# The last step of the first network: its function cut into three chunks, its adds moved, and the order of three engines written out up to the second network

## The chip, the cores and the metric

The kernel runs on one core of a Trainium2 chip, in one launch. The metric is the device time of that core in microseconds (us), as the median of several executions. The engines named here are TensorE (PE, matrix products into PSUM; its weight loads are shown as PEld), VectorE (DVE), ScalarE (ACT), GpSimd (POOL) and SyncE (SP, which issues the DMAs).

## The reference

Three stages run one behind the other: an attention with random features over 2 batches, 8 heads, 576 positions; a first network; a second network. Its output, 1152 tokens of 512 values, goes through

```python
def _moe_ref(x, w_in, w_out):          # x 1152 x 512, w_in 512 x 2048, w_out 2048 x 512
    h = x @ w_in
    g = h - np.tanh(h)
    return (g @ w_out).astype(np.float32)

def _moe2_ref(x, domain_probs, w1, w2): # 4 experts, w1 512 x 1024, w2 1024 x 512
    p = domain_probs / (domain_probs.sum(-1, keepdims=True) + 1e-09)
    for e in range(E):
        h = np.maximum(x @ w1[e], 0.0)
        out += p[:, e:e + 1] * (h @ w2[e])
```

All products need near float32 precision. The kernel splits each operand into a high part in the fp32r format and a low part (operand minus high part), and adds three products for one: high by high, high by low, low by high.

## The kernel before

**First network.** Tokens lie along the free axis, 1152 wide, in three chunks of 384 (`NC = 3`, `CH = 384`). The 2048 hidden values are 16 blocks of 128, four units (i) of four blocks (j). For a block, `hidden` makes 36 matmuls into one PSUM tile `psh` of three banks (one bank a chunk). `activated` then computes h - tanh(h) from `psh` as ten operations, named by letters: on ScalarE `u` (h squared), `q`, `t` (tanh), `m` (mask of small h), `h` (high part `hh`); on VectorE `a`, `b` (a polynomial for small h), `s` (h - tanh h, in place in PSUM), `c` (the predicated copy that takes the polynomial where the mask is 0 or not), `l` (low part `hl`). Each of them runs over all 1152 tokens. `out_a(i, c, n)` makes the 12 matmuls that a unit adds to output rows c (of 4), tokens n (of 3), into a PSUM tile `po`; the function that it returns adds `po` to `acc` on VectorE (L550). There are two `po` buffers, so a third product waits for the add of the first.

**The loop.** Step n of twelve issues the hidden block `sh` (units 1 to 3) and the output row block `so` (of the unit before), three `out_a`. In the last step `sh` is block (3, 3) and `so` is (2, 3). Around it run the function of the block before, here (3, 2), and the weights' split: `Decoded` weights of this network arrive as float64, `y` and `m` on ScalarE (L111, L117) and two operations on VectorE (L126, L127) make a float32 `m` of them, ScalarE its high part and GpSimd its low part `wbl`. In this loop the order on VectorE, ScalarE and TensorE is the order in which the code emits (`manual_schedule`); in the last step the first two adds (`o[:1]`, `o[1:2]`) stand around the predicated copy `c`, as in all steps.

**Behind the loop.** The function of block (3, 3) runs whole. Of the last unit's twelve products the first five are begun with three of their four blocks (`last[:5]`): three in a spare `psh` tile, one bank each, two in `po`. When `hh` and `hl` of (3, 3) are there, the five get their last three matmuls each, all five in a row. Then the hand-written order ends. What comes next is placed by the framework's scheduler: the five adds, the split of `acc` into the second network's input (`x2`: high part on ScalarE, low part on VectorE, chunk by chunk), the other seven products, the first hidden blocks of the second network (`psh<-y`, weights `wah` and `wal` split from `raw` by ScalarE and VectorE), sums of tokens T1 to T4 (L568, `token_sums`), weights' sums (L598). The scheduler may move these up into the loop where an engine has room: the four weight splits `wah`, `wal` stand in the steps before, and 11 matmuls of the second network stand ahead of the sixth output product.

**Second network.** Experts' blocks 0 and 1 are plain (`hidden`, `activated`, `out_b` at L665); from the third pair on a Strassen scheme runs, hand-ordered again. The change doesn't touch it.

Of the kernel before, what the change touches and what calls it, by code (L numbers as in the profile page):

```python
# [8 lines left out]
F32 = mybir.dt.float32  # L9
F32R = mybir.dt.float32r  # L10
# [16 lines left out]
def tile_favor_attention__then__two_moe(  # L27
# [46 lines left out]
    def run(todo):  # L74
        for step in todo:
            step()
# [21 lines left out]
    class Decoded:  # L98
# [30 lines left out]
        def parted(self):  # L129
            hi, lo = halves_of(wp, self.tag)  # L130
            split(hi, lo, self.m.bitcast(F32), nc.gpsimd)
            return hi, lo
# [339 lines left out]

    def early(e):
# [224 lines left out]
    def opened(w):  # L698
        for x, _, _ in w:
            x.scaled()  # L700
            x.topped()
# [4 lines left out]
    with tc.manual_schedule(engines={mybir.EngineType.DVE, mybir.EngineType.PE, mybir.EngineType.Activation}):  # L706
# [3 lines left out]
        for n, (sh, so) in enumerate(order):  # L710
            now, coming = coming, loads(n + 1)
            g0 = g
            run(g0[x] for x in "uqt" if g0)
            edge = so % NJ == 0 and g0 is not None
# [11 lines left out]
            else:  # L726
                o, late_h = [], sh == END - 1
                run(H if late_h else H[:2])
                for c in range(NC):
                    o.append(out_a(*steps[so], c))  # L730
                    run(H[2 + c:3 + c] if not late_h else [])
                run(J[:1] + W[:1] + left + T("a") + T("m") + T("b") + T("s") + o[:1] + T("c") + T("h"))
                run(J[1:] + W[1:] + o[1:2] + T("l"))
            left = o[2:]
            g = activated(*steps[sh])
            opened(coming)
        last = [(c, n) for n in range(NC) for c in range(KD)]
        spare = late["ps_ha"].tile([P, NC, 512], F32, tag="h", name="psh")
        run(g[x] for x in "uqt")
        coming[0][0].joined()  # L740
        parted(*coming[0])
        run(left + [g[x] for x in "amb"])
        for k, (c, n) in enumerate(last[:5]):
            out_a(NA - 1, c, n, range(NJ - 1), spare[:, k] if k < NC else None)
        run(g[x] for x in "schl")
        ends = {(c, n): out_a(NA - 1, c, n, [NJ - 1]) for c, n in last[:5]}
    for f in range(2):
        ready(load_a, wa, NA, f)
    x2 = [[xp.tile([P, N], F32R, tag=f"x{a}{c}", name=f"y{a}{c}") for a in range(2)] for c in range(KD)]
    for n in range(NC):  # L750
        s = slice(n * CH, (n + 1) * CH)
        for c in range(KD):
            (ends.get((c, n)) or out_a(NA - 1, c, n))()
            split(x2[c][0][:, s], x2[c][1][:, s], state["acc"][:, c, s])
        if n == 1:
            state["x"] = x2
            for j in range(2):
                hidden(NA, j, [0])
# [155 lines left out]
```

## Time and profile before

| | us |
|---|---|
| median of 3 runs (lowest, highest) | 685.01 (684.14, 686.36) |
| the profiled execution | 686.23 |
| its span | 684.4 |
| TensorE busy | 668.2 (98%) |
| VectorE busy | 528.5 (77%) |
| ScalarE busy | 317.2 (46%) |
| GpSimd busy | 61.3 (9%) |

The span is from the first to the last instruction on the core; 1.8 us of the profiled execution lie outside it. TensorE is busy nearly all the time, so it is read by the few places where it waits. A timeline row gives the start, the time, the engine, the line and operation, the output tile and the inputs, the number of instructions of the row, and in brackets the idle time before it and what ended it. Matmuls overlap: the time of one (0.34 us for 384 columns) is longer than the distance from one start to the next (0.173 us).

### The profile page before, as it was taken

The page shows a single profiled execution, that of the slowest core. Times are in us where ns is not written, and L with a number is a line of the kernel's source. Part 1 is how long each engine was busy: PE and PEld are TensorE (multiplying, and loading weights), DVE is VectorE, ACT ScalarE, POOL GpSimd, SP SyncE. Part 2 cuts the span into 40 slices and gives each one's busy share as a digit, 9 for nine tenths or more (in the row PEclk, how much of TensorE's full clock was granted, in tenths as well). Part 3 has the DMA queues.
Part 4 walks back from the last instruction along what each step waited for, and adds up shares of the span by engine and source line. Part 5 has one row for each costly group of instructions (what it writes and reads, how often), then busy time and mean ns, then how long its engine had stood idle before and what let it go on. Part 6 is the DMA issues. An engine that isn't in the chain of part 4 may idle for free.

```text
span 684.4 us, 10149 instructions
## 1 busy us (share of the span) xinstructions
PE 668.2 (98%) x4059; PEld 622.5 (91%) x4059; DVE 528.5 (77%) x824; ACT 317.2 (46%) x591; POOL 61.3 (9%) x58
## 2 busy tenths in 40 slices
PE   6999999999999999899999999999999999999997
PEld 5899989999999999799898899999988999999996
DVE  3599989799999977769477777777776878777664
ACT  4699988857757655435022222322232222232120
POOL 1032113413212200000000000000000000000000
PEclk9999999999999999999999999999999999999999
DMA  8853211012212222011001102120201110110004
GB/s 224 259 171 113 87 32 32 32 61 94 93 62 92 78 78 63 31 32 49 13 32 62 33 31 62 32 62 32 63 31 59 35 62 32 32 61 1 1 0 139
DMA packets 42767, 43.73 MB, mean 64 GB/s; under 512 B 5600, under 2 KB 37600, under 8 KB 42720
## 3 DMA queue, kind: packets, MB, share of 16 engines
q1 hardware_dynamic: 42720, 43.08, 20.2%
q8 instruction: 32, 0.52, 0.3%
q14 instruction: 15, 0.12, 0.1%
HBM read 40.72 MB, written 2.36 MB: 63 GB/s over the span
## 4 chain that ended last, share of the span: by engine, by line
PE 77%; DVE 13%; ACT 5%; issue 2%; DMA 2%; SPq 1%; DVEq 0%
PE po L665 29%; PE Y L648 23%; PE psh L437 7%; PE po L544 6%; PE pse L437 4%; PE psP L296 3%; PE psN L348 2%; DVE y L454 2%; DVE y L451 1%; DVE y L452 1%; DVE psh L453 1%; ACT y L448 1%; DVE m L127 1%; DVE m L126 1%; ACT m L117 1%
## 5 line engine op out<-in xcount | busy, mean ns | idle before, releaser
L671 DVE SCALAR_TENSOR_TENSOR oacc<-po,pr,oacc 128x512 f32<-128x512 f32 (+1 forms) x136 | 101.3, 746 | 34.2 <-PE po L665 33.8
L665 PE MATMUL po<-wbh,hl 128*128 128x512 f32 x290 | 113.0, 389 | 0.4 <-DVE hl L468 0.4
L665 PE MATMUL po<-wbh,hh 128*128 128x512 f32 x290 | 112.9, 389 | 0.1
L665 PE MATMUL po<-wbl,hh 128*128 128x512 f32 x290 | 112.9, 389 | 0.0
L665 PEld LDWEIGHTS po<-wbh,hl 128*128 128x128 f32 x290 | 54.4, 188 | 12.2 <-DVE hl L468 0.8
L665 PEld LDWEIGHTS po<-wbh,hh 128*128 128x128 f32 x290 | 54.7, 189 | 8.2 <-DVE oacc L671 0.3
L665 PEld LDWEIGHTS po<-wbl,hh 128*128 128x128 f32 x290 | 54.4, 188 | 7.5
L544 PE MATMUL po<-hh,wbh 128*128 128x384 f32 x180 | 60.8, 338 | 0.3
L826 ACT ACTIVATE hh<-Y 128x576 fp32r<-128x576 f32 x42 | 27.4, 653 | 72.5 <-DVE Y L823 64.0
L544 PE MATMUL po<-hh,wbl 128*128 128x384 f32 x180 | 60.5, 336 | 0.5 <-POOL wbl L72 0.5
L544 PE MATMUL po<-hl,wbh 128*128 128x384 f32 x180 | 60.7, 337 | 0.3 <-DVE hl L456 0.2
L648 PE MATMUL Y<-y,wah 128*128 128x288 f32 x336 | 57.9, 294 | 0.0
L437 PE MATMUL psh<-x,wah 128*128 128x384 f32 x288 | 57.7, 336 | 0.0
L648 PEld LDWEIGHTS Y<-y,wah 128*128 128x128 f32 x336 | 51.2, 188 | 3.6 <-DVE hl L468 0.3
L437 PEld LDWEIGHTS psh<-x,wah 128*128 128x128 f32 x288 | 50.5, 188 | 0.0
L648 PE MATMUL Y<-Th,wal 128*128 128x288 f32 x224 | 47.8, 295 | 0.0
L648 PE MATMUL Y<-Tl,wah 128*128 128x288 f32 x224 | 47.6, 294 | 0.0
L648 PE MATMUL Y<-Th,wah 128*128 128x288 f32 x224 | 47.6, 293 | 0.0
L826 ACT ACTIVATE hh<-u 128x576 fp32r<-128x576 f32 x14 | 9.6, 687 | 73.5 <-DVE u L823 73.5
L648 PEld LDWEIGHTS Y<-Th,wah 128*128 128x128 f32 x224 | 39.0, 188 | 4.5
L455 ACT ACTIVATE hh<-y 128x1152 fp32r<-128x1152 f32 (+3 forms) x24 | 20.3, 846 | 45.2 <-DVE y L454 45.2
L618 ACT ACTIVATE wah<-y 128x512 fp32r<-128x512 f32 x28 | 17.6, 631 | 41.1 <-DVE y L598 41.1
(138 smaller groups left out, 1472.5 us busy)
## 6 DMA issues: line engine op xcount, KB each, us to landing
raw<-in_moe_w_dram SPq DMA_DIRECT2D x30, 512.0 KB, 3.5
raw<-in_moe_w_in_dram SPq DMA_DIRECT2D x16, 512.0 KB, 3.6
raw<-in_moe_w_out_dram SPq DMA_DIRECT2D x16, 512.0 KB, 3.4
kn<-in_k_dram SPq DMA_DIRECT2D x8, 256.0 KB, 4.1
vs<-in_v_dram SPq DMA_DIRECT2D x8, 256.0 KB, 4.6
qn<-in_q_dram SPq DMA_DIRECT2D x8, 256.0 KB, 4.9
out_dram<-oacc SPq DMA_DIRECT2D x7, 256.0 KB, 2.3
raw<-in_moe_w_dram SPq DMA_DIRECT2D x4, 256.0 KB, 3.5
```

The source lines that it names most:

```text
L117: nc.scalar.activation(m, self.low.bitcast(U32), AF.Copy, scale=2.0**-29 * (1 - 2.0**-18), bias=-0.49999)
L296: nc.tensor.matmul(ps[:, i].rearrange("p a m -> p (a m)"), x[:, c], o, start=j == 0, stop=j == 2)
L348: nc.tensor.matmul(ps[:, j, h, :ZC], qt[g][:, j, h, :], kvz[p][:, t // (TB + 1), h, :], start=True, stop=True)
L437: nc.tensor.matmul(ph[i, j][:, n, :CH] if bank is None else bank, w[:, c], x[:, n * CH:(n + 1) * CH] if bank is None else x[:, n], start=z ...
L454: c=lambda: vec.copy_predicated(view(y), view(u).bitcast(I32), ps),
L455: h=lambda: act.activation(hh, y, AF.Copy),
L544: nc.tensor.matmul(po[:, :CH], w[:, r], g[:, s], start=j == 0 and z == 0, stop=j == NJ - 1 and z == 2,)
L618: nc.scalar.activation(w[0], src, AF.Copy)
L648: nc.tensor.matmul(ps[:, m, :HN // 2], w[:, kk], b[:, m * HN // 2:(m + 1) * HN // 2], start=first and kk == 0 and z == 0, stop=kk == 1 and ...
L665: nc.tensor.matmul(po, g[:, s], w[:, cols], start=j == 0 and z == 0, stop=j == 1 and z == 2)
L671: nc.vector.scalar_tensor_tensor(out=acc, in0=po, scalar=pr[:, t, e:e + 1], in1=acc, op0=ALU.mult, op1=ALU.add)
L826: nc.scalar.activation(halves(gs[NA + q, f][0][:, h * HN:(h + 1) * HN]), x, AF.Relu)
```

## The change

The function of the last block (3, 3) is made by a new helper, `activated_by_chunk`, as three sets of the ten operations, 384 tokens each. In the last step the two weight splits of the second network's first blocks (`plain_w`) and the `y` and `m` of the last weight are emitted right behind `u`, `q`, `t` of block (3, 2); the adds are emitted behind `c`, `h`, `l`. The hand-written order goes on to the end of the `x2` split: each of the five begun products gets its last three matmuls, then its add, high part, and (one later) low part, one product at a time; then the seven others; and the second network's first 24 matmuls stand behind the eighth product. A scheduling barrier keeps the scheduler from moving later work above that point. No matmul, DMA or split is added or removed; VectorE has ten rows more and the same elements.

```diff
--- before.py
+++ after.py
@@ -468,6 +468,16 @@
             lambda: nc.vector.scalar_tensor_tensor(
                 out=grid(hl), in0=ps, scalar=0.0, in1=grid(hh).bitcast(F32), op0=ALU.max, op1=ALU.subtract
             ),
+        ]
+
+    def activated_by_chunk(i, j):
+        new_g(i, j)
+        hh, hl = gs[i, j]
+        t, u, y = (late["gp"].tile([P, N], F32, tag=z, name=z, bufs=1 + (z == "y")) for z in "tuy")
+        cut = [slice(n * CH, (n + 1) * CH) for n in range(NC)]
+        return [
+            minus_tanh(ph[i, j][:, n, :CH], hh[:, s], hl[:, s], t[:, s], u[:, s], y[:, s], lambda z: z, None)
+            for n, s in enumerate(cut)
         ]
 
     def early(e):
@@ -711,6 +721,11 @@
             now, coming = coming, loads(n + 1)
             g0 = g
             run(g0[x] for x in "uqt" if g0)
+            final = sh == END - 1
+            if final:
+                for x in plain_w:
+                    parted(*x)
+                opened(coming)
             edge = so % NJ == 0 and g0 is not None
             H = [lambda kk=kk: hidden(*steps[sh], kks=[kk]) for kk in range(KD)]
             T = (lambda x: [g0[x]]) if g0 else (lambda x: [])
@@ -724,38 +739,54 @@
                 o = [out_a(*steps[so], c, [NJ - 1]) for c in range(2)] + [out_a(*steps[so], 2)]
                 run(o[:2])
             else:
-                o, late_h = [], sh == END - 1
-                run(H if late_h else H[:2])
+                o = []
+                run(H if final else H[:2])
                 for c in range(NC):
                     o.append(out_a(*steps[so], c))
-                    run(H[2 + c:3 + c] if not late_h else [])
-                run(J[:1] + W[:1] + left + T("a") + T("m") + T("b") + T("s") + o[:1] + T("c") + T("h"))
-                run(J[1:] + W[1:] + o[1:2] + T("l"))
+                    run(H[2 + c:3 + c] if not final else [])
+                run(J[:1] + W[:1] + left + T("a") + T("m") + T("b") + T("s") + ([] if final else o[:1]) + T("c") + T("h"))
+                run(J[1:] + W[1:] + (T("l") + o[:2] if final else o[1:2] + T("l")))
             left = o[2:]
-            g = activated(*steps[sh])
-            opened(coming)
+            if not final:
+                g = activated(*steps[sh])
+                opened(coming)
+            if n == len(order) - 2:
+                plain_w = [(load_a(NA, f), wa, (NA, f)) for f in range(2)]
+
+        g = activated_by_chunk(*steps[END - 1])
         last = [(c, n) for n in range(NC) for c in range(KD)]
         spare = late["ps_ha"].tile([P, NC, 512], F32, tag="h", name="psh")
-        run(g[x] for x in "uqt")
+        run(g[0][x] for x in "uqt")
+        run(left)
         coming[0][0].joined()
+        run(g[1][x] for x in "uqt")
         parted(*coming[0])
-        run(left + [g[x] for x in "amb"])
-        for k, (c, n) in enumerate(last[:5]):
-            out_a(NA - 1, c, n, range(NJ - 1), spare[:, k] if k < NC else None)
-        run(g[x] for x in "schl")
-        ends = {(c, n): out_a(NA - 1, c, n, [NJ - 1]) for c, n in last[:5]}
-    for f in range(2):
-        ready(load_a, wa, NA, f)
-    x2 = [[xp.tile([P, N], F32R, tag=f"x{a}{c}", name=f"y{a}{c}") for a in range(2)] for c in range(KD)]
-    for n in range(NC):
-        s = slice(n * CH, (n + 1) * CH)
-        for c in range(KD):
-            (ends.get((c, n)) or out_a(NA - 1, c, n))()
-            split(x2[c][0][:, s], x2[c][1][:, s], state["acc"][:, c, s])
-        if n == 1:
-            state["x"] = x2
-            for j in range(2):
-                hidden(NA, j, [0])
+        for z, (c, n) in enumerate(last[:5]):
+            out_a(NA - 1, c, n, range(NJ - 1), spare[:, z] if z < NC else None)
+        run(g[0][x] for x in "ambsc")
+        run(g[2][x] for x in "uq")
+        g[0]["h"]()
+        g[2]["t"]()
+        for n in range(1, NC):
+            g[n]["a"]()
+            g[n - 1]["l"]()
+            run(g[n][x] for x in "mbsch")
+        g[NC - 1]["l"]()
+        x2 = [[xp.tile([P, N], F32R, tag=f"x{a}{c}", name=f"y{a}{c}") for a in range(2)] for c in range(KD)]
+        low = []
+        for z, (c, n) in enumerate(last):
+            s = slice(n * CH, (n + 1) * CH)
+            out_a(NA - 1, c, n, range(NJ - 1, NJ) if z < 5 else range(NJ))()
+            src, (hi, lo) = state["acc"][:, c, s], (x[:, s] for x in x2[c])
+            nc.scalar.activation(hi, src, AF.Copy)
+            run(low)
+            low = [lambda src=src, hi=hi, lo=lo: nc.vector.tensor_tensor(out=lo, in0=src, in1=hi.bitcast(F32), op=ALU.subtract)]
+            if z == 2 * KD - 1:
+                state["x"] = x2
+                for f in range(2):
+                    hidden(NA, f, [0])
+        run(low)
+    tc.no_sync_barrier()
     for n in range(1, NC):
         for j in range(2):
             hidden(NA, j, [n])
```

Three places, as the order of the built programs shows them (names: `wal`, `wah` are the second network's first weights, `wal` VectorE's low part and `wah` ScalarE's high part; `m` the decoded weights, `acc` the adds, `hl` the low part of a block).

VectorE before, from the weights' operations of the last step to the low part of block (3, 2):

```order
L126 SCALAR_TENSOR_TENSOR m<-y,m 128x512
L72 TENSOR_TENSOR wal<-raw,wah 128x512
L127 SCALAR_TENSOR_TENSOR m<-raw,m 128x512
L550 TENSOR_TENSOR acc<-po,acc 128x384
L451 SCALAR_TENSOR_TENSOR y<-y,u 128x1152
L452 SCALAR_TENSOR_TENSOR y<-y,psh 128x1152
L453 TENSOR_TENSOR psh<-psh,t 128x3x384
L550 TENSOR_TENSOR acc<-po,acc 128x384
L454 COPY_PREDICATED y<-u,psh 128x1152
L550 TENSOR_TENSOR acc<-po,acc 128x384
L598 TENSOR_TENSOR y<-raw 128x256
L456 TENSOR_TENSOR hl<-y,hh 128x1152
```

VectorE now, from the low part of block (3, 1) to the adds of the last step:

```order
L456 TENSOR_TENSOR hl<-y,hh 128x1152
L72 TENSOR_TENSOR wal<-raw,wah 128x512 x2
L126 SCALAR_TENSOR_TENSOR m<-y,m 128x512
L127 SCALAR_TENSOR_TENSOR m<-raw,m 128x512
L560 TENSOR_TENSOR acc<-po,acc 128x384
L451 SCALAR_TENSOR_TENSOR y<-y,u 128x1152
L452 SCALAR_TENSOR_TENSOR y<-y,psh 128x1152
L453 TENSOR_TENSOR psh<-psh,t 128x3x384
L454 COPY_PREDICATED y<-u,psh 128x1152
L456 TENSOR_TENSOR hl<-y,hh 128x1152
L560 TENSOR_TENSOR acc<-po,acc 128x384 x3
```

The two `wal` come ahead of everything else of the step, and the three adds come behind `hl`, where before one stood before the predicated copy and one behind it.

ScalarE before, from `u` of block (3, 2):

```order
L447 ACTIVATE u<-psh 128x1152
L448 ACTIVATE y<-u,ca 128x1152
L449 ACTIVATE t<-psh 128x1152
L71 ACTIVATE wbh<-m 128x512
L450 ACTIVATE u<-u,ct 128x1152
L455 ACTIVATE hh<-y 128x1152
L111 ACTIVATE y<-raw 128x512
L117 ACTIVATE m<-raw 128x512
```

ScalarE now, from the same instruction:

```order
L447 ACTIVATE u<-psh 128x1152
L448 ACTIVATE y<-u,ca 128x1152
L449 ACTIVATE t<-psh 128x1152
L71 ACTIVATE wah<-raw 128x512 x2
L111 ACTIVATE y<-raw 128x512
L117 ACTIVATE m<-raw 128x512
L71 ACTIVATE wbh<-m 128x512
L450 ACTIVATE u<-u,ct 128x1152
L455 ACTIVATE hh<-y 128x1152
L447 ACTIVATE u<-psh 128x384
```

The two `wah`, which stood in earlier steps, and `y`, `m` of the last weight now stand between `t` and `wbh`.

TensorE before, last matmuls of the five begun products (`psh_3195` is the spare tile of three banks, `hh_3186` and `hl_3187` the parts of block (3, 3)), with what waits:

```order
L544 MATMUL psh_3195<-hh_3186,wbh_2960 128x384 [waits Activation_49]
L544 MATMUL psh_3195<-hl_3187,wbh_2960 128x384 [waits DVE_49]
L544 MATMUL psh_3195<-hh_3186,wbl_2961 128x384
L544 MATMUL psh_3195<-hh_3186,wbh_3066 128x384
L544 MATMUL psh_3195<-hl_3187,wbh_3066 128x384
L544 MATMUL psh_3195<-hh_3186,wbl_3067 128x384
L544 MATMUL psh_3195<-hh_3186,wbh_3172 128x384
```

TensorE now, the same matmuls (`psh_3207` the spare tile, `hh_3202`, `hl_3203` the parts):

```order
L554 MATMUL psh_3207<-hh_3202,wbh_2960 128x384 [waits Activation_49]
L554 MATMUL psh_3207<-hl_3203,wbh_2960 128x384 [waits DVE_49]
L554 MATMUL psh_3207<-hh_3202,wbl_2961 128x384
L554 MATMUL psh_3207<-hh_3202,wbh_3066 128x384 [waits DVE_49]
L554 MATMUL psh_3207<-hl_3203,wbh_3066 128x384
L554 MATMUL psh_3207<-hh_3202,wbl_3067 128x384
L554 MATMUL psh_3207<-hh_3202,wbh_3188 128x384 [waits DVE_49]
```

The matmuls are the same; the second and the third product of the spare tile now begin with a wait for VectorE, which stood nowhere in this piece but at the first `hl`. In the program these two waits are for the add (L560) of the first and of the second product, which is emitted before them and reads the same tile, in another bank.

## Rows read from the trace of the kernel before

**Rows 1.** The page, part 1: busy time, share, instructions.
```profile
PE 668.2 (98%) x4059; PEld 622.5 (91%) x4059; DVE 528.5 (77%) x824; ACT 317.2 (46%) x591; POOL 61.3 (9%) x58
```

**Rows 2.** Who TensorE waited for, 225 to 345 us: total, times, longest.
```profile
PE psh L544 <- ACT hh L455: 1.2, 1, 1.2
PE psh L544 <- DVE hl L456: 1.0, 1, 1.0
PE po L544 <- POOL wbl L72: 0.5, 1, 0.5
PE po L665 <- DVE hl L468: 0.4, 1, 0.4
```

**Rows 3.** Timeline of VectorE in the last step: start, us, instruction, idle before.
```profile
257.04 1.35 DVE L456 TENSOR_TENSOR hl<-y,hh 128x1152 fp32r<-128x1152 f32 x1
258.31 0.68 DVE L126 SCALAR_TENSOR_TENSOR m<-y,m 128x512 int32<-128x512 int32 x1
258.91 0.68 DVE L72 TENSOR_TENSOR wal<-raw,wah 128x512 fp32r<-128x512 f32 x1
...
263.40 1.36 DVE L453 TENSOR_TENSOR psh<-psh,t 128x1152 f32<-128x1152 f32 x1
268.53 0.56 DVE L550 TENSOR_TENSOR acc<-po,acc 128x384 f32<-128x384 f32 x1 [3.76 <-PE po L544]
```

**Rows 4.** Timeline of ScalarE in the last step.
```profile
261.53 0.62 ACT L71 ACTIVATE wbh<-m 128x512 fp32r<-128x512 f32 x1
...
270.54 1.17 ACT L455 ACTIVATE hh<-y 128x1152 fp32r<-128x1152 f32 x1 [7.21 <-DVE y L454]
```

**Rows 5.** Timeline of TensorE, start of the second network's output.
```profile
314.38 0.43 PE L665 MATMUL po<-wbh,hh 128*128 128x512 f32 x1
...
316.40 0.47 PE L665 MATMUL po<-wbh,hh 128*128 128x512 f32 x1
```

**Rows 6.** Timeline of VectorE in an earlier step, copy directly behind its subtraction.
```profile
225.96 1.36 DVE L453 TENSOR_TENSOR psh<-psh,t 128x1152 f32<-128x1152 f32 x1
227.42 1.52 DVE L454 COPY_PREDICATED y<-u,psh 128x1152 f32<-128x1152 int32 x1
228.82 0.69 DVE L126 SCALAR_TENSOR_TENSOR m<-y,m 128x512 int32<-128x512 int32 x1
229.55 0.69 DVE L127 SCALAR_TENSOR_TENSOR m<-raw,m 128x512 int32<-128x512 int32 x1
```

**Rows 7.** Timeline of TensorE, last step and end of the first network.
```profile
270.41 0.34 PE L544 MATMUL po<-hh,wbh 128*128 128x384 f32 x1
...
272.49 0.34 PE L544 MATMUL psh<-hh,wbh 128*128 128x384 f32 x1
...
286.69 1.28 PE L437 MATMUL psh<-y,wah 128*128 128x384 f32 x3 [0.16 <-ACT y L71]
```

**Rows 8.** Timeline of VectorE, 384-wide adds in a row.
```profile
285.52 1.49 DVE L550 TENSOR_TENSOR acc<-psh,acc 128x384 f32<-128x384 f32 x3 [1.77 <-PE psh L544]
```

**Rows 9.** Timeline of ScalarE, 384-wide copies in a row.
```profile
286.11 1.45 ACT L71 ACTIVATE y<-acc 128x384 fp32r<-128x384 f32 x3 [3.75 <-DVE acc L550]
```

**Rows 10.** Stretches: length, busy us by engine (instructions), granted clock, DMA.
```profile
280.00:282.50 2.50, 1.30 (x8) 0.98 (x7) 1.27 (x2) 1.16 (x1) 0.00 (x0) 1.00 0.00 0
680.50:681.00 0.50, 0.21 (x2) 0.01 (x1) 0.25 (x1) 0.00 (x0) 0.00 (x0) 1.00 0.91 340
682.50:683.00 0.50, 0.00 (x0) 0.00 (x0) 0.00 (x0) 0.00 (x0) 0.00 (x0) 0.61 0.05 14
```

**Rows 11.** Timeline of TensorE at the start of the kernel.
```profile
8.04 0.45 PE L284 MATMUL psT<-ident,kr 128*128 128x128 f32 x1 [2.64 <-DMA kr<-in_k_dram]
...
11.06 0.63 PE L296 MATMUL psP<-ob,th 128*128 128x256 f32 x2
...
13.87 0.48 PE L296 MATMUL psP<-ob,th 128*128 128x256 f32 x2
...
16.31 0.39 PE L296 MATMUL psP<-ob,th 128*128 128x256 f32 x2
```

## Prediction

> **What bounds the kernel now.** I read part 1 of the page first: TensorE is busy 668.2 of 684.4 us [rows 1], so all its idle time is 16.2 us, and a change that leaves its matmuls alone can give back only waits, or add some. Then the list of waits for the stretch of the change: four of any size, 1.2, 1.0, 0.5 and 0.4 us [rows 2]. Then the timelines, to see what stands ahead of each. In the last step VectorE is through with the subtraction `s` (it starts at 263.40) and idles 3.76 us until TensorE has the first product of the step, because its add stands ahead of the predicated copy [rows 3]; ScalarE gets the copy's result so late that it idles 7.21 us before `hh` at 270.54 [rows 4]. The function of the last block is late by that, and TensorE waits for its `hh` and `hl`. So VectorE's chain through the last two blocks bounds this place, and its program order decides.
>
> **The change, step by step.** I follow VectorE and TensorE on the clock of the profiled execution, up to one TensorE instruction that both kernels have: the first matmul with `hh` of the second network's block 1, at 316.40 before [rows 5]. All matmuls up to it are the same.
>
> *The weights hold VectorE.* Two `wal` now stand ahead of all of VectorE's work of the last step. They need the two `wah`, and those stand on ScalarE behind `t`. ScalarE leaves `t` for its next 512-wide copy at 261.53 and takes 0.62 us for it [rows 4], so the first `wah` is there at 262.15. VectorE is free at 258.31 [rows 3]: it stands 3.9 us. Behind it queue the weights' decoding, the add of the step before and the whole function of block (3, 2). The two `wal` are 0.60 us apart, like the decode and the `wal` in [rows 3]; the decode starts at 263.4. From decode to `s` it was 5.09 us with one `wal` in between [rows 3], so 4.5 without it, and I add 0.1 for the decode's second half, which now follows its first directly: `s` at 268.0. Copy 1.46 behind it and 1.52 long [rows 6]: ends 270.9, where before it ended at 270.5. The move of the adds gains nothing here; the weights have eaten it. `hh` 1.17 [rows 4]: 272.1. `hl`: the next instruction can start 1.27 us behind its start [rows 3], at 273.4.
>
> *The adds behind it hold TensorE.* Only there stands the first add, 0.56 us [rows 3]: done at 274.0. The third product of the step needs its buffer; before it began at 270.41 without a wait [rows 7]. New stall: 3.6 us. What was VectorE's wait for TensorE becomes TensorE's wait for VectorE.
>
> *The chunked function.* The third product takes 2.08 us, from 270.41 to 272.49 before [rows 7]; with restart and reading its add starts at 276.4. Then the decode of the last weight, 0.73 and 0.63 us [rows 6]: `a` of the first chunk at 278.2. No row has the function at 384 wide. Its adds are 0.56 us, 0.47 apart ([rows 8], three in 1.49); ScalarE's copies 0.53, 0.46 apart ([rows 9], three in 1.45); an operation on the result of the one before it costs 0.1 us more than that one's length (1.46 against 1.36, [rows 6]). The 384-wide predicated copy lies between 0.56 [rows 8] and the full 1.52 [rows 6]; I take 0.58, since its width is that of the adds. So the first copy ends at 280.6. On ScalarE `u` and `q` of the third chunk stand ahead of the first chunk's `hh`, and `u` waits for that copy, which reads the same tile: `hh` 282.2, `hl` 282.8. Second chunk: copy 284.4, `hh` 285.0, `hl` 285.5. Third: copy 287.2, `hh` 287.7, `hl` 288.3. These 10.1 us take the place of one pass over 1152 tokens, some 8 us: cutting a row of dependent operations in three saves no work. Then the first add of a finished product: 288.2 to 288.8.
>
> *The finished products, one at a time.* TensorE has 45 matmuls of the five begun products behind the third one, 7.8 us at 0.173 each, to 284.0; the first chunk is there, and the first product's last three take it to 284.5. The second product lies in the same tile and now waits for the first's add, at 288.8: stall 4.3 us. The third waits for the second's add, 0.8 us; the sixth for the buffer of the fourth, whose add stands behind two low parts and two adds, 0.7 us. Before, all 15 matmuls ran in a row, and 11 of the second network from 286.69 on [rows 7] covered the wait for buffers; that cover is gone, since they now stand behind the eighth product. The sixth product starts at 292.5.
>
> *To the end of the stretch.* From there 156 matmuls without a wait, 27.0 us: 319.5, where before it was 314.38 [rows 5]. The last product ends at 311.2; add, high and low part put VectorE at 313.0, with four token sums (1.27 us each, 1152 wide like `hl`), two `wal` and two `wbl` (0.6) ahead of the first hidden block's `hl`, so 320.5. On ScalarE its `hh` stands behind a token part that waits for the third of these sums. I get 0.7 us of wait for `hh` and 0.7 for `hl`, where before it was 0.4 for `hl` [rows 2]: 0.85 more with restarts. So 322.4 against 316.40: 6.0 us later. The waits of [rows 2] are gone within that sum; it is made on the clock, not by adding them.
>
> *Edits at nothing.* The last weight's DMA now goes out behind two others, but as soon as its buffer is free, some ten microseconds ahead of its use. Four small weight sums of 0.4 us leave the loop for the stretch behind 325 us, where VectorE has gaps between its adds; the later hand-ordered part is the same, and TensorE carries the delay to the end. If the gaps don't hold them, up to 1.7 us.
>
> *The clock.* Before, it read 1.00 at the 1.2 us wait [rows 10]. Two stalls of 3.6 and 4.3 us are longer than any of TensorE's waits before. Behind the last matmul, near 680.7, the granted clock was 0.61 of full in 682.5 to 683.0 [rows 10], which is on the way to the lower level, 1.2 GHz. And behind the 2.64 us wait at 8.04 two matmuls of 256 columns took 0.63 us at 11.06, and 0.39 at 16.31 [rows 11]: half speed for 3.0 to 5.8 us. The price of a fall is so between 0 and 2.9 us, half of that time; behind the longer stall part of it lies in waits for adds. Slowed matmuls put the sixth product at 293.6 and cost 0.3 more behind it: I take 1.4. Behind the first stall it would be 2.0, since the slowed third product delays the add.
>
> The Trainium skill (TensorE: Matmul & The Clock Gate, Part 1: The HAM clock gate) says that the array's clock is cut to half by default and that activity releases it, between two states only. By that rule each of the two stalls may cost, and the sum is the one with both falls, below. The trace agrees at the end of the kernel [rows 10] and has no such stall in its middle.
>
> **Sum.** 6.0 + 1.4 = 7.4 us on the profiled execution's 686.23 (span 684.4 and 1.8 outside it), 693.6; that execution is 1.2 above the median, so 692.4.
>
> **The rivals.** *The clock stays.* For it: 1.00 at the shorter waits. Against: the fall at the end. 691.0. *It falls in both stalls.* 6.0 + 2.0 + 1.4 = 9.4: 694.4. *VectorE isn't held by the weights*, because `wah` is early after all: then the first add is at 268.5 as now, the first stall is gone and the chain is 3.6 us earlier, but the second product still waits for the first's add: +2.4, 687.4. Against it: both queues run in program order, and ScalarE's place for `wah` is behind `t`. *Faster:* the chunked function is short enough that the add of the first product is done when TensorE gets to the second, which needs VectorE not held and the 10.6 us from `a` to that add down to about 6; decisive is whether that add ends by 281. Then the waits of [rows 2] but the last go, with their restarts, some 4.4 us between 270.41 and 314.38 (43.97 us for 228 matmuls of 0.173): 680.6. For it: `hh` of the first third is early. Against it: the add of the first product stands on VectorE behind the `hl` of the third chunk.
>
> **How the numbers follow.** One fall 0.40, none 0.30, both 0.20, not held 0.06, faster 0.04. What a measurement of this kernel tells from no change is 0.3%, 2.05 us. All of the first three are slower, and half of "not held"; the other half and a quarter of "faster", should it come in small, are no change: 0.93 slower, 0.04 same, 0.03 faster. The range goes from 688.5, between "not held" and "clock stays", to 695.3, above both falls: the unknown copies alone can add 2.8 us, and the gaps 1.7.
>
> **What would show it.** TensorE waits 3 to 4 us for L560 before the last step's third product and 4 us before the second product's last three; VectorE idles near 4 us before the first `wal`, for ScalarE; the granted clock under 1.00 behind 285. Wrong would be: no idle time of VectorE before `wal`, or the second product starting with the first's add still open, or a stretch of under 46 us from the third product to the second network's first output.

## The result, and the profile after

| kernel | median of the runs | lowest to highest |
|---|---|---|
| before | 684.71 us | 684.14 to 686.36 |
| changed | 694.30 us | 693.53 to 695.19 |

The ratio is 1.0137, with a 95% interval of 1.0115 to 1.0158: slower by 9.6 us. That is inside the forecast range, and the sign is right; but of the cases it is not the likeliest (692.4, the clock falls in one stall), it is the rival in which it falls in both (694.4). Two executions, 1338.98 us of the kernel with late splits below (the one that was traced) and 3766.58 of the kernel before, lie far outside the others and are in no ratio.

The profiled execution of the changed kernel took 694.05 us with a span of 692.2. Part 1 of its page, against [rows 1]:

```profile
PE 672.0 (97%) x4059; PEld 626.1 (90%) x4059; DVE 529.9 (77%) x834; ACT 318.7 (46%) x601; POOL 62.1 (9%) x58
```

The same 4059 matmuls are busy 3.8 us longer, and TensorE is idle for 692.2 - 672.0 = 20.2 us where it was 16.2. The first number is matmuls that take longer; the second is waits, of which those at the kernel's start were 1.7 us fewer in this execution (below). Who TensorE waited for from 225 to 350 us (total, times, longest), against [rows 2]:

```profile
PE psh L554 <- DVE acc L560: 4.8, 2, 4.1
PE po L554 <- DVE acc L560: 3.3, 1, 3.3
PE po L675 <- ACT hh L467: 0.5, 1, 0.5
PE po L675 <- DVE hl L468: 0.5, 1, 0.5
```

The three waits for `hh`, `hl` and `wbl` of [rows 2] are gone, as meant. In their place stand 8.1 us of waits for the adds of L560. VectorE, against [rows 3]:

```profile
255.32 1.35 DVE L456 TENSOR_TENSOR hl<-y,hh 128x1152 fp32r<-128x1152 f32 x1
260.46 1.29 DVE L72 TENSOR_TENSOR wal<-raw,wah 128x512 fp32r<-128x512 f32 x2 [3.79 <-ACT wah L71]
...
266.13 1.36 DVE L453 TENSOR_TENSOR psh<-psh,t 128x1152 f32<-128x1152 f32 x1
267.59 1.50 DVE L454 COPY_PREDICATED y<-u,psh 128x1152 f32<-128x1152 int32 x1
...
271.60 1.02 DVE L560 TENSOR_TENSOR acc<-po,acc 128x384 f32<-128x384 f32 x2
275.93 0.56 DVE L560 TENSOR_TENSOR acc<-po,acc 128x384 f32<-128x384 f32 x1 [3.32 <-PE po L554]
...
277.73 0.55 DVE L451 SCALAR_TENSOR_TENSOR y<-y,u 128x384 f32<-128x384 f32 x1
...
287.30 0.56 DVE L456 TENSOR_TENSOR hl<-y,hh 128x384 fp32r<-128x384 f32 x1 [0.59 <-ACT hh L455]
287.78 0.55 DVE L560 TENSOR_TENSOR acc<-psh,acc 128x384 f32<-128x384 f32 x1
```

`hl` starts at 255.32, in [rows 3] at 257.04: everything in this execution is 1.72 us early when the step begins. TensorE's waits up to 225 us, nearly all at the kernel's start, add up to 8.6 us in the trace before and to 6.8 here; the wait of 2.64 for the transfer of `kr` [rows 11] is not among them. So 1.72 has to be added before a time is held against the prediction. The hold ahead of `wal` is 3.79, the first add comes only behind `hl`, and VectorE is itself idle for 3.32 us before the third add: it waits for the product that it has held up. TensorE in the same stretch, against [rows 7]:

```profile
272.20 0.69 PE L554 MATMUL po<-hh,wbh 128*128 128x384 f32 x1 [3.35 <-DVE acc L560]
272.69 0.52 PE L554 MATMUL po<-hl,wbh 128*128 128x384 f32 x1
273.01 0.52 PE L554 MATMUL po<-hh,wbl 128*128 128x384 f32 x1
...
275.38 0.34 PE L554 MATMUL po<-hl,wbh 128*128 128x384 f32 x1
275.56 0.34 PE L554 MATMUL po<-hh,wbl 128*128 128x384 f32 x1
275.73 0.34 PE L554 MATMUL psh<-hh,wbh 128*128 128x384 f32 x1
...
288.38 0.44 PE L554 MATMUL psh<-hh,wbh 128*128 128x384 f32 x1 [4.14 <-DVE acc L560]
...
290.04 0.69 PE L554 MATMUL psh<-hh,wbh 128*128 128x384 f32 x1 [0.65 <-DVE acc L560]
...
293.46 0.53 PE L554 MATMUL po<-hl,wbh 128*128 128x384 f32 x1
293.78 0.53 PE L554 MATMUL po<-hh,wbl 128*128 128x384 f32 x1
```

Read the distances of the starts: 0.32 us behind the first wait (272.69 to 273.01), 0.17 further on (275.38 to 275.56), and 0.32 again behind the second (293.46 to 293.78), down to 295.38. That is the granted clock, by stretches (length, busy us of the five engines, clock, DMA share, GB/s), which [rows 10] show at 1.00 in the waits of before:

```profile
270.00:272.00 2.00, 0.00 (x0) 0.00 (x0) 1.68 (x2) 1.97 (x5) 0.00 (x0) 0.93 0.00 0
272.00:274.00 2.00, 1.80 (x6) 1.80 (x7) 0.61 (x2) 1.07 (x3) 0.00 (x0) 0.50 0.03 8
276.00:278.00 2.00, 2.00 (x13) 2.00 (x12) 1.97 (x4) 0.09 (x1) 0.00 (x0) 1.00 0.00 0
286.00:288.00 2.00, 0.00 (x0) 0.00 (x0) 1.31 (x4) 0.52 (x1) 0.00 (x0) 1.00 0.00 0
288.00:290.00 2.00, 1.00 (x3) 0.48 (x3) 0.91 (x3) 0.52 (x1) 0.00 (x0) 0.70 0.00 0
292.00:294.00 2.00, 2.00 (x8) 1.80 (x7) 2.00 (x5) 1.12 (x3) 0.00 (x0) 0.50 0.00 0
```

It fell to 1.2 GHz (0.50) at the end of the first wait, and a second time just behind the second wait. The stretch ends here, against [rows 5]:

```profile
322.06 0.50 PE L675 MATMUL po<-wbh,hh 128*128 128x512 f32 x1 [0.55 <-ACT hh L467]
...
323.75 0.50 PE L675 MATMUL po<-wbh,hl 128*128 128x512 f32 x1 [0.49 <-DVE hl L468]
...
324.27 0.39 PE L675 MATMUL po<-wbh,hh 128*128 128x512 f32 x1
```

324.27 + 1.72 = 325.99 against 316.40: 9.59 us later, which is the whole difference. From here to the last matmul both kernels need the same.

### The profile page after: what moved, and what is told of

Same layout as the page of the kernel before. It is cut to its first block, busy times and chain, and to the rows that moved or that the text cites. A ratio compares the mean times of both kernels' runs of the same rounds, so it can differ in the third digit from the quotient of the medians.

```text
span 692.2 us, 10171 instructions
## 1 busy us (share of the span) xinstructions
PE 672.0 (97%) x4059; PEld 626.1 (90%) x4059; DVE 529.9 (77%) x834; ACT 318.7 (46%) x601; POOL 62.1 (9%) x58
## 4 chain that ended last, share of the span: by engine, by line
PE 76%; DVE 13%; ACT 6%; issue 2%; DMA 1%; SPq 1%; DVEq 0%; ACTq 0%
PE po L675 28%; PE Y L658 22%; PE po L554 7%; PE psh L437 6%; PE pse L437 4%; PE psP L296 3%; PE psN L348 2%; DVE y L454 2%; DVE y L452 2%; DVE psh L453 2%; DVE m L127 1%; DVE y L451 1%; DVE m L126 1%; ACT y L448 1%; ACT u L447 1%
## 5 line engine op out<-in xcount | busy, mean ns | idle before, releaser
L554 PE MATMUL po<-hh,wbh 128*128 128x384 f32 x180 | 62.5, 347 | 3.6 <-DVE acc L560 3.3
L554 PE MATMUL po<-hl,wbh 128*128 128x384 f32 x180 | 62.1, 345 | 0.2 <-DVE hl L456 0.2
L554 PEld LDWEIGHTS po<-hh,wbh 128*128 128x128 f32 x180 | 35.0, 194 | 5.1 <-DVE acc L560 4.8
```

The source lines that it names most:

```text
L554: nc.tensor.matmul(po[:, :CH], w[:, r], g[:, s], start=j == 0 and z == 0, stop=j == NJ - 1 and z == 2,)
```

## The experiments

To compare kernels whatever their start was, I take from each trace the length of one stretch: from the first matmul of the last step's first product to the first matmul of the second network's output that takes `hl` (the one at 323.75 above). Before it is 49.64 us, in the changed kernel 323.75 - 264.53 = 59.22, +9.58. The ratios are to runs of the kernel before on the same chip.

| kernel | median us | ratio, 95% interval | stretch against before |
|---|---|---|---|
| changed: late splits | 689.42 | 1.0061 (1.0046 to 1.0075) | not read |
| changed: adds back | 690.47 | 1.0081 (1.0065 to 1.0097) | +5.01 |
| changed: last matmuls in a row | 692.08 | 1.0106 (1.0090 to 1.0121) | +7.43 |
| changed: late splits and in a row | 687.88 | 1.0042 (1.0025 to 1.0058) | +3.82 |
| the same at full width | 687.18 | 1.0024 (1.0013 to 1.0035) | +2.97 |
| changed: first wait filled | 693.63 | 1.0124 (1.0110 to 1.0138) | +9.42 |
| changed: both filled | 696.14 | 1.0165 (1.0147 to 1.0183) | +11.64 |
| changed: both filled, shorter | 690.96 | 1.0083 (1.0067 to 1.0100) | +6.31 |
| before: adds moved alone | 684.13 | 0.9988 (0.9977 to 0.9998) | -0.97 |
| before: splits early alone | 689.87 | 1.0064 (1.0048 to 1.0081) | +4.79 |
| adds and splits spread | 682.69 | 0.9966 (0.9955 to 0.9978) | -2.38 |
| spread, fifth product early | 680.55 | 0.9929 (0.9912 to 0.9946) | -3.52 |

**Who makes the first wait: the splits, the adds' place, or both.** Three trials. First the splits alone are undone (its trace is not read here; the kernel with this edit and another, below, shows the waits):

```diff
             if final:
-                for x in plain_w:
-                    parted(*x)
                 opened(coming)
...
+            if final:
+                for x in plain_w:
+                    parted(*x)
             left = o[2:]
```

> The changed kernel with one edit: the two splits of the second network's weights (copy `wah` on ScalarE, subtraction `wal` on VectorE) go back from the head of the last step to behind its adds. Theory (these splits hold VectorE 3.8 us, that makes TensorE wait 3.35 us ahead of the step's third product, and the clock that falls in that wait costs 1.45 us more): VectorE's idle time ahead of `wal` and TensorE's first wait are gone, the third product's matmuls are 0.17 us apart from the first on, the second wait of some 4 us behind the first finished product stays with its fall of the clock; 694.3 - 4.8 = 689.5 us. Rival (the adds' new place behind the predicated copy and `hl` makes the first wait by itself): the wait stays within 1 us of 3.35, and the time at 693.5 to 694.5.

689.42, as the theory says (689.5); the rival is out. Then the splits stay and the adds go back:

```diff
-                run(J[:1] + W[:1] + left + T("a") + T("m") + T("b") + T("s") + ([] if final else o[:1]) + T("c") + T("h"))
-                run(J[1:] + W[1:] + (T("l") + o[:2] if final else o[1:2] + T("l")))
+                run(J[:1] + W[:1] + left + T("a") + T("m") + T("b") + T("s") + o[:1] + T("c") + T("h"))
+                run(J[1:] + W[1:] + o[1:2] + T("l"))
```

> The changed kernel with one edit: in the last step the adds go back to where they stood before, the first ahead of the predicated copy, the second ahead of `hl`; the splits stay at the head of the step. Nothing else moves, since the order around it is by hand here, where the trial with the kernel before had other weights' splits drawn into the step. Theory (the hold of 3.8 us lies in VectorE's wait for the first product when the add stands ahead of the copy, and only hold and new place together make TensorE wait): the idle time ahead of `wal` stays at 3.8 us, the first add comes right behind `s`, TensorE's wait of 3.35 us and its fall of the clock go, the third add comes at 272.0 instead of 275.9, and the second wait grows by some 1.0: 694.3 - 3.95 = 690.3 us, 689.5 to 691. Rival (the hold alone makes the function late by its whole length, and TensorE pays for it later): 693 to 694.5.

690.47 against 690.3 expected. VectorE there:

```profile
260.36 1.29 DVE L72 TENSOR_TENSOR wal<-raw,wah 128x512 fp32r<-128x512 f32 x2 [3.79 <-ACT wah L71]
...
266.02 1.36 DVE L453 TENSOR_TENSOR psh<-psh,t 128x1152 f32<-128x1152 f32 x1
267.29 0.55 DVE L560 TENSOR_TENSOR acc<-po,acc 128x384 f32<-128x384 f32 x1
267.75 1.50 DVE L454 COPY_PREDICATED y<-u,psh 128x1152 f32<-128x1152 int32 x1
```

The hold is the same 3.79 us, but the add follows `s` at once: the product it waits for is there by now, so the hold lies where VectorE waited before anyway. TensorE's only larger waits are then the two at the finished products:

```profile
284.20 0.69 PE L554 MATMUL psh<-hh,wbh 128*128 128x384 f32 x1 [4.77 <-DVE acc L560]
286.18 0.69 PE L554 MATMUL psh<-hh,wbh 128*128 128x384 f32 x1 [0.65 <-DVE acc L560]
```

So each of the two edits alone leaves the first wait out, and both together make it. The hold isn't quite free even so: the step's third add starts 7.35 us behind the start of the stretch here, and 6.45 in the kernel below with late splits and the last matmuls in a row.

The third trial put the splits early into the kernel before, with a scheduler still filling in around the hand order:

> The kernel before with the other part of the change alone: the two splits of the second network's weights at the head of the last step, ahead of all of VectorE's work, the adds where they were. Theory (VectorE is held 3.9 us there, but behind it stands the add that waits until 268.5 for the first product anyway, so the hold lies inside that wait; neither part costs much alone, and only the adds' new place behind the held function makes the hold TensorE's wait): VectorE's idle time moves from ahead of the add to ahead of `wal`, the predicated copy comes 0 to 0.6 us later, 684.5 to 685.8 us. Rival (the hold costs its full length in either order): 688 or more.

The theory fell, and the number is on the rival's side: 689.87. But the hold is not what it shows. With the splits early, their buffers came free early, and the order drew two more splits of the second network's weights and their transfers into the step. VectorE, ahead of `b` (L452):

```profile
264.24 1.79 DVE L72 TENSOR_TENSOR wal<-raw,wah 128x512 fp32r<-128x512 f32 x1
265.95 1.34 DVE L452 SCALAR_TENSOR_TENSOR y<-y,psh 128x1152 f32<-128x1152 f32 x1
```

I had left out what moves by itself. The trial ahead of it, with the orders around it by hand, answers the question; this one leaves it open.

**The other part alone.** The adds moved behind the copy in the kernel before, without the splits:

> The kernel before with one part of the change alone: in the last step the adds stand behind the predicated copy, `hh` and `hl`. Theory (the idle time of VectorE ahead of its add in the last step makes the last block's function late, and TensorE's waits of 1.2, 1.0 and 0.5 us behind it): VectorE's 3.8 us idle ahead of `acc` goes, the third product still starts without a wait, since its add is done near 269.5 on the clock of the kernel before and it starts at 270.4; TensorE's waits in the stretch shrink by 2 to 3 us, 681.7 to 682.7. Rival (something else ends last there, such as the last weight or ScalarE): 684 to 685, the waits as they were. Second rival (the third product now waits for the add): slower than 685.

684.13: less than expected, on the rival's side. The 3.8 us idle are gone, yet the last block's `hl` is only 1.0 us earlier on the clock of before. The trace has where the rest went: VectorE now idles 0.93 us for `hh` (0.24 before) and 0.83 for the second product, and one weight sum of 256 columns, 0.42 us elsewhere, takes 1.53 here. VectorE first, then GpSimd at the same time:

```profile
271.12 0.42 DVE L598 TENSOR_TENSOR y<-raw 128x256 f32<-128x256 f32 x1
...
271.92 1.35 DVE L451 SCALAR_TENSOR_TENSOR y<-y,u 128x1152 f32<-128x1152 f32 x1
273.19 1.53 DVE L598 TENSOR_TENSOR y<-raw,y 128x256 f32<-128x256 f32 x1
```

```profile
260.99 1.30 POOL L72 TENSOR_TENSOR wbl<-m,wbh 128x512 fp32r<-128x512 f32 x1 [11.18 <-ACT wbh L71]
272.06 2.37 POOL L72 TENSOR_TENSOR wbl<-m,wbh 128x512 fp32r<-128x512 f32 x1 [9.77 <-ACT wbh L71]
```

GpSimd's `wbl` takes 1.07 us more than the one at 260.99, about as long as VectorE's `a` runs on beside it (to 273.27); the sum behind `a` ends 0.3 us behind `wbl` and is 1.11 us longer than the one at 271.12. The rows read as if the two took turns.

**The second wait.** The last matmuls of the five begun products in a row again:

```diff
+        ends = [out_a(NA - 1, c, n, [NJ - 1]) for c, n in last[:5]]
...
-            out_a(NA - 1, c, n, range(NJ - 1, NJ) if z < 5 else range(NJ))()
+            (ends[z] if z < 5 else out_a(NA - 1, c, n))()
```

> The changed kernel with one edit: the last three matmuls of all five begun products stand in a row ahead of the five adds, as they did before the change. Theory (the second product waits for the first one's add only because they share a PSUM tile, but the sixth product needs the buffer of the fourth, and VectorE is not free for any add before the third chunk's `hl`): the wait does not go, it moves to the head of the sixth product, which starts near 291 instead of 293.1, with more matmuls at the low clock behind it: 0.5 to 2 us less, 692.3 to 693.8. Rival (the shared tile is the whole second wait): the wait of 4.1 us and its clock loss go, 688 to 689.

692.08, 0.2 below the theory's range and far from the rival: the wait moved to the sixth product and shrank from 4.14 and 0.65 to 3.90.

```profile
290.46 0.69 PE L554 MATMUL po<-hh,wbh 128*128 128x384 f32 x1 [3.90 <-DVE acc L560]
```

With both edits:

> The changed kernel with both edits: the splits of the second network's weights behind the last step's adds, and the last matmuls of the five begun products in a row. Theory (two waits one behind the other, each with its own fall of the clock, so the gains add up): 4.8 and 0.5 to 2 us less, 687.5 to 689; still above the kernel before, by what the chunked function and the missing cover of matmuls cost. Rival (the chunked function costs nothing, the two waits are all there is): 684 or less.

687.88, as expected, and TensorE has one wait left before the second network's output, with its fall of the clock (granted 0.50 from 286 to 292 us):

```profile
286.70 0.69 PE L554 MATMUL po<-hh,wbh 128*128 128x384 f32 x1 [4.62 <-DVE acc L560]
```

Now the function of the last block in one pass:

```diff
-        g = activated_by_chunk(*steps[END - 1])
+        g = activated(*steps[END - 1])
...
+        run(g[x] for x in "ambschl")
```

> The changed kernel with late splits and the last matmuls in a row, and with the last block's function over all 1152 tokens at once instead of in three chunks. Theory (three chunks make VectorE's chain from the first `a` to the last `hl` 10.1 us long, one pass some 8.2): the first add of a finished product comes 1.1 us earlier, the wait of 4.6 us splits into one of some 2.3 for `hl` and one of some 1.4 for the add, and the clock falls less or not: 687.9 - 1.1 to - 3.4, so 684.5 to 686.8. Rival (the chunks help, since the first third of `hh` and `hl` is early): 688 or more.

687.18, between the theory (686.8 at most) and the rival (688 or more): a gain of 0.7, by the stretch 0.85. The chain is shorter as worked out, `hl` is there 1.9 us earlier than the chunks' last; but the first add is not:

```profile
280.36 1.36 DVE L456 TENSOR_TENSOR hl<-y,hh 128x1152 fp32r<-128x1152 f32 x1 [1.23 <-ACT hh L455]
283.49 1.02 DVE L560 TENSOR_TENSOR acc<-psh,acc 128x384 f32<-128x384 f32 x2 [1.77 <-PE psh L554]
```

TensorE gets `hl` late, finishes three products in one tile, and only then may the first of them be added. What VectorE saves it waits for: with chunks and without, the first add starts 18.30 us and the sixth product 21.46 us behind the start of the stretch. So the 2 us for cutting the function in three are real on VectorE, and no later start comes of them here. The 0.85 us lie behind that point: the granted clock, 0.50 from 286 to 292 us with chunks, reads 0.82, 0.50 and 0.82 in the three stretches of 2 us from 286 to 292 at full width, and fewer matmuls are slow.

**The clock.** The disputed term is measured by keeping TensorE busy in both waits with matmuls into columns that nothing reads:

```diff
+                    if final and c == 1:
+                        for _ in range(48):
+                            nc.tensor.matmul(po_of[(steps[so][0], steps[so][1], 1)][:, CH:512], ..., start=True, stop=True)
...
+            if z == 1:
+                for _ in range(72):
+                    nc.tensor.matmul(po_of[NA - 1, 3, 0][:, CH:512], ..., start=False, stop=False)
```

> The changed kernel with 48 matmuls of 128 columns added on TensorE between the last step's second and third product, where it now waits 3.35 us for the add; they write columns that nothing reads, so nothing else waits for them. At 128 of 384 columns of 0.173 us each they take some 2.8 us. Theory (the third product's matmuls are 0.32 us apart because the clock fell while TensorE stood still): the granted clock reads 1.00 from 270 to 276, the third product's matmuls are 0.17 apart from the first on, its 2.1 us instead of 3.5 pass on to VectorE and the end: 694.3 - 1.45 = 692.9 us. Rival (the spacing has another cause, such as VectorE or ScalarE at work beside it): spacing 0.32 as before and 694.3, or more if the added matmuls are in the way.

693.63, where 692.9 was expected, and both together:

> As with the first wait filled, and 72 more such matmuls between the last three of the first begun product and the last three of the second, where TensorE now waits 4.1 us; they too write columns that nothing reads. Theory (both waits cost their own length, and beside it a fall of the clock): the granted clock stays at 1.00 through the whole stretch, and the time is that of the forecast's rival without a fall, 691.0 us, 690.8 to 691.6, since the added matmuls can run over the end of a wait by some tenths. Rival (only the first wait's fall costs time, the second one's lies in waits for adds): 692.5 to 693.

696.14, where 691.0 was expected. Both fillings were too long: 48 matmuls of 128 columns took 5.30 us, 0.110 each, where I had taken a third of 0.173. The granted clock did stay at 1.00, but the third product started 1.8 us late. The counts were corrected to 29 and 36:

> Both waits of the changed kernel filled as before, but with fewer matmuls, so that they end ahead of the wait's end: a matmul of 128 columns took 5.30 / 48 = 0.110 us in the runs with fills and not 0.058, and so the first filling ended 1.8 us too late and the second 3. Now 29 (3.2 us into a wait of 3.35) and 36 (4.0 us into one of 4.1). Theory (the fall of the clock costs 1.45 us behind the first wait and 0.9 + 1.0 behind the second, the waits themselves the rest): granted clock 1.00 throughout, the third product's start within 0.3 us of its place in the changed kernel, and 694.3 - 3.4 = 690.9 us, 690.4 to 691.5. Rival (a clock that stays up gives nothing back, since VectorE's chain sets the end): 693.5 to 694.5.

690.96 against 690.9. The third product starts 7.69 us behind the first one's start, in the changed kernel 7.67: same place, other clock. TensorE there, and the granted clock behind the second wait:

```profile
268.86 3.35 PE L749 MATMUL po<-hh,wbh 128*128 128x128 f32 x29
272.39 0.44 PE L554 MATMUL po<-hh,wbh 128*128 128x384 f32 x1 [0.18 <-DVE acc L560]
```

```profile
290.00:292.00 2.00, 1.46 (x9) 1.14 (x8) 2.00 (x6) 1.07 (x3) 0.00 (x0) 1.00 0.00 0
```

So of the 9.6 us 694.30 - 690.96 = 3.3 are the two falls of the clock, and 6.3 the waits and what hangs on them (the stretch is +6.31). The traces split the 3.3: the matmul that ends the second wait starts 23.85 us behind the start of the stretch in the changed kernel and 22.54 here, so 1.3 belong to the first fall and the other 2.0 to the second.

**A version that beats both.** The experiments say what to do: keep the first add behind the copy, put the other adds and the splits where VectorE waits for ScalarE, and finish a product early whose buffer is wanted next.

```diff
-            left = o[2:]
+            left = o[1:] if final else o[2:]
...
+        last = last[3:4] + last[:3] + last[4:]
+        g["a"]()
+        run(left[:1])
+        run(g[x] for x in "mb")
+        run(left[1:])
...
+        run(g[x] for x in "sc")
+        parted(*plain_w[0])
+        g["h"]()
+        g["l"]()
+        parted(*plain_w[1])
```

> A version meant to beat both: the loop's last step with the first add behind the predicated copy and `hl`; the second and third add and the two `wal` spread over the places where VectorE waits in the last block's function; that function at full width; the fourth begun product finished first, so that the sixth product's buffer is free; the last matmuls in a row; the weight sums behind the stretch as in the changed kernel. Theory (VectorE's order is all that made TensorE wait there): `hl` of the last block is ready before TensorE is through with the begun products, its waits of 1.2, 1.0 and 0.5 us and their restarts go, the tail costs 0.9 more: 681.5 us, 680.6 to 682.5. Rival (another engine ends last, ScalarE's 512-wide copies or GpSimd's `wbl`): 684 to 686.

682.69, 0.2 above the range: faster than before, with one wait left before the second network's output, 0.84 us at the seventh product. One more edit, the fifth product finished and added early as well:

```diff
-        last = last[3:4] + last[:3] + last[4:]
+        last = last[3:5] + last[:3] + last[5:]
...
-        for z, (c, n) in enumerate(last[1:4] + last[:1] + last[4:5]):
+        for z, (c, n) in enumerate(last[2:5] + last[:2]):
```

> The version with the adds and splits spread over VectorE's waits, with one more edit: of the five begun products the fourth and the fifth are finished and added first, and the three that share a PSUM tile behind them. Theory (its one wait left, 0.84 us at the seventh product, is for the add of the fifth, which stood behind three adds and three low parts): that wait and its restart of 0.3 go: 682.7 - 1.1 = 681.6 us, 681.0 to 682.2. Rival (the adds of the other three come later now, and the wait moves to the second network's first matmuls or to the eighth product): 682.4 to 683.0.

680.55, ratio 0.9929 (0.9912 to 0.9946), below the expected 681.0 to 682.2. By the stretch the edit gave what was worked out: 47.26 - 46.12 = 1.14 us, against 1.1. Against the kernel before, the stretch is 3.52 us shorter. The other 1.4 us of the 4.9 lie ahead of it, since behind it both kernels need 364.5 us to the last matmul; why is not shown (the traces reach the stretch at 263.71 to 266.25 us). TensorE's waits from 225 to 350 us are now the two at the second network's output alone, 0.5 us each. The second network's first matmuls stand behind the eighth product in this kernel as well, so the cover that they gave before isn't needed where the adds come early enough.

## Why the prediction was right, and where it was not

Step by step, times of the changed kernel with 1.72 added.

- *The weights hold VectorE:* 3.9 us forecast, 3.79 measured; `s` at 267.85 (268.0), the copy's end at 270.81 (270.9), the second add's end at 274.3, the first add so at about 273.9 (274.0). Right, and shown by the two trials with one edit undone.
- *The adds hold TensorE:* 3.6 forecast, 3.35 measured.
- *The chunked function:* from `a` of the first chunk to the first add of a finished product 10.0 us forecast (278.2 to 288.2), 287.78 - 277.73 = 10.05 measured. It began 1.25 us later than forecast, since the slowed third product delayed the add before it. For the predicated copy at 384 wide the text took 0.58 and called it unknown; it took 0.58 to 0.60, and the trace before already had four copies of that width elsewhere, 0.60 us each.
- *The finished products:* 4.3 and 0.8 us forecast, 4.14 and 0.65 measured. The 0.7 at the sixth product is not there in the changed kernel: slowed matmuls cover it. It is there with the clock up (0.54 in the trial with both waits filled).
- *To the end of the stretch:* 0.7 and 0.7 forecast, 0.55 and 0.49 measured.
- *The clock:* this is the term that was mis-sized. "I take 1.4", for a fall in the second stall alone; it fell in both, and cost 3.3. What failed is the choice of the case: one fall had 0.40 and both 0.20, without a row that told the two stalls apart. [rows 10] pointed the other way: the clock read 0.61 in a stretch that begins 1.8 us behind the last matmul, and the first stall was forecast at 3.6 us. The price of both falls, 2.0 + 1.4 = 3.4, met the 3.3 in part by luck: the first cost 1.3 (the third product took 275.73 - 272.20 = 3.53 us, with the clock up 274.58 - 272.39 = 2.19) and the second 2.0. Nor do [rows 11] show a price for a fall, as the text reads them: ahead of the wait at 8.04 four matmuls of 128 columns took 1.11 us at 4.28, and at 16.65 eight took 1.05, so TensorE was at half speed before that wait too. The profile's granted clock reads 1.00 from 2 to 18 us and so doesn't follow the matmuls there.

The Trainium skill (TensorE: Matmul & The Clock Gate, Part 1: The HAM clock gate) gives the clock of a single busy core two states only, half and full, and the rows of this stretch agree: 0.50 or 1.00 wherever they lie on one side of a change. By that rule both stalls could cost, and that was the right case.

- *Edits at nothing:* the four weight sums moved behind the stretch cost nothing: from the end of the stretch to the last matmul it is 364.50 us, before 364.55.
- The rival *not held* was priced as the loss of the hold alone, 687.4. Measured is 689.42 with late splits: the second stall then has its own fall of the clock, which that price left out.
- The rival *faster* said 680.6, if all of TensorE's waits but the last could go. The last version measured 680.55. That the numbers meet is in part luck: the rival has 4.4 us in the stretch, the last version 3.5 there and 1.4 ahead of it. But most of the gain was there, and the change's own order is what missed it.

## What to carry to other kernels

Before a consumer is moved behind a longer chain, ask what else is added ahead of that chain: here each of two edits was covered by the same wait, or nearly so, and together they had no cover. Where stalls of TensorE as long as these (3.35 and 4.14 us) are forecast, price the fall of the clock behind each of them, and look for a wait in which VectorE can do the displaced work. Where a scheduler fills in around a hand order, a trial that frees a buffer early tests what it pulls in as well.

## What the runs showed of the hardware that I had not expected

- The clock also fell where no wait was as long as those two. With the function at full width TensorE waited 0.96, 0.95 and 2.16 us, one soon behind the other; it had already begun again at 286.65 when the clock fell. The stretches there:

```profile
286.00:288.00 2.00, 1.34 (x6) 1.35 (x7) 2.00 (x5) 1.18 (x3) 0.00 (x0) 0.82 0.00 0
288.00:290.00 2.00, 2.00 (x8) 2.00 (x7) 0.00 (x0) 0.09 (x1) 0.00 (x0) 0.50 0.00 0
```

- A matmul of 128 columns, each with its weight load, took 0.110 us, one of 384 columns 0.173: not in proportion. Why is not shown.
- VectorE and GpSimd stopped each other: a sum of 0.42 us took 1.53 and a subtraction of 1.30 took 2.37 in the same place. The Trainium skill (SBUF — State Buffer, Who interferes with whom) says that the two share a pair of ports as a lock, so that one stands while the other finishes. The rows of the kernel with the adds moved alone agree, with 1.11 and 1.07 us; in the changed kernel a `wbl` beside VectorE's `a` (263.47 to 264.82) took 2.04 at 263.95.
